# Decaying attention with a soft mixture of experts: the order of the turns in the score half of a pass, and a copy of the tokens' turns

## The chip, the cores and the metric

The kernel runs on one core of a Trainium2 chip, in one launch. The metric is the device time of an execution in microseconds. A core has TensorE (matrix products, here PE, and PEld for its weight loads), VectorE (DVE), ScalarE (ACT), GpSimd (POOL) and SyncE (SP), which issues all DMAs of this kernel. Each engine takes its instructions in the order of the program and stops at one whose inputs or whose buffer isn't ready; a semaphore tells it when they are. Products land in PSUM, which has 8 banks of 512 f32 columns on 128 partitions.

## The reference

All of it is computed in f32 (products partly in the fp32r form, with a second product for the low part):

```python
# attention: q, k, v [8, 8, 576, 64], f [8, 8, 576]
scores = q @ k.T / sqrt(64)
cum = cumsum(log(clip(f, 1e-4, 1)), -1)
scores = where(causal, -1e9, scores + cum[..., :, None] - cum[..., None, :])
attn = exp(scores - scores.max(-1))
attn = attn / (attn.sum(-1) + 1e-9)
x = (attn @ v).transpose(0, 2, 1, 3).reshape(4608, 512)
# soft mixture of experts: phi [512, 32], w1 [8, 512, 1024], w2 [8, 1024, 512]
logits = x @ phi
d = exp(logits - logits.max(0)); d /= d.sum(0) + 1e-9      # over tokens
slot_input = (d.T @ x).reshape(8, 4, 512)
slot_out[e] = relu(slot_input[e] @ w1[e]) @ w2[e]          # for each expert
c = exp(logits - logits.max(1)); c /= c.sum(1) + 1e-9      # over slots
out = c @ slot_out
```

## The kernel before

The 64 heads go through in 32 pairs, g = 0 to 31, four pairs to a batch of 576 tokens. Pair 0 has code of its own; pairs 1 to 31 run through the loop at line 714, one pass each, and its body is an order written out by hand: the lines are issued to the engines as they stand. In a pass the kernel

- makes the scores of the pair's heads h0 = 2g and h1 = 2g + 1 with keys on partitions (`s2`: two products for a segment, into three banks `ring` in turn), takes their exponential on ScalarE out of the bank (`expo`, one for each of four banks of a head) and lets GpSimd mask the diagonal blocks (`causal`);
- makes, between these, another form of scores for heads u0 = 2g + 3 and u1 = 2g + 4, with queries on partitions (`s1`, into three banks `s` in turn), out of which VectorE takes each query's maximum (`tops`: a masked maximum and then a reading of the accumulator). TensorE transposes the maxima of pair g + 1 (`mturn`, when u0's are there), ScalarE copies them (`mrows`), and a DMA puts them as a row into the operand `YA`, so that `s2` of the next pass subtracts them;
- turns the outcome of the pair before, g - 1: `px` transposes the five blocks of 128 tokens (t = 0 to 4, the last of 64 tokens) from tokens to channels, into two banks, `pv[0]` (blocks 0 and 3) and `pv[1]` (blocks 1, 2 and 4), and `xcopy` copies them on ScalarE to `XT`. These are the turns of channels;
- ends with 100 value products (`s3`) into the same two banks, `pv[0]` for h0 and `pv[1]` for h1, and `norm` on VectorE divides them by their sums, which frees the banks.

Columns 325 to 452 of these banks, beside the values, hold further small things: block 4's turn in `pv[1]`, and in `pv[0]` the transposes of `mturn` and `mtop`.

```python
    TURN = {0: (0, 0), 1: (1, 0), 2: (1, 128), 4: (1, 325), 3: (0, 128)}
```

The experts' routing of batch b is spread over the four passes behind it, by w = (g - 4) mod 4: in w = 0 the logits are made (`logits`, behind `s3`); in w = 1 their running maximum (`weigh`, `mgroup`, `mtop`, `mcast`) and the exponentials (`weigh2`), and behind `s3` `tokens` turns the logits (160 columns) and the negated maxima (32 columns) to tokens on partitions, into one of the three `s` banks. In w = 2 VectorE reads that bank: `combine(b, 0)` takes the maximum over the slots and subtracts it (lines 502 and 503), `shift` adds the maxima to the logits (468 and 470), and ScalarE takes the exponential (471); `dispatch` multiplies the outcome `LD` with the tokens in 40 products ahead of `s3`. In w = 3 the combining weights are made ready. Passes with w = 0 and 3 and the first three have nothing of this between the first score product and `s3`.

SP's queue loads values, queries and keys for later passes and in passes 5 to 27 a 512 KB quarter of the experts' weights each. From pass 28 on the buffers of the attention become free one by one, and the other weights are loaded into them (`wstream`). Behind the loop come the last batch's routing, the experts and the output.

Of the kernel before, what the change touches and what calls it, by code (L numbers as in the profile page):

```python
# [72 lines left out]
def attn_softmoe(ctx: ExitStack, tc: tile.TileContext, qk, v, f, phi, w1, w2, cst, out):  # L73
# [41 lines left out]

    mk = const.tile([P, NE], F32, name="mk")
    one = const.tile([1, 4], F32, name="one")
    under = const.tile([P, NS], F32, name="under")
    MT = [const.tile([P, 2 * NBLK], F32, name=f"MT{i}") for i in range(3)]


# [95 lines left out]
    def s1(i, *which):  # L217

        if not head(i):
            return  # L220
        g, h = divmod(i, 2)
        ya, wa, m = YA[g % 3], WA[g % 3][:, S * h : S * h + S], TOP[g % 3]
        for n in which:
            bank, o, blk, j0, w = TOPS[n]
            if o == 0:
                st["top", i % 2, bank] = scratch(False, f"s{i}_{bank}")
            t = st["top", i % 2, bank]
            nc.tensor.matmul(  # L228
                t[:, o : o + w], ya[0:m, h, 128 * blk : 128 * blk + 128], wa[0:m, j0 : j0 + w], start=True, stop=True
            )  # L230

    def tops(i, *which):
        if not head(i):
            return
        g, h = divmod(i, 2)
        for n in which:
            bank, o, blk, j0, w = TOPS[n]
            t = st["top", i % 2, bank]
            m0 = max(448 - (128 * blk + 64) + j0, 0)
            top = MT[g % 3][:, NBLK * h + blk : NBLK * h + blk + 1] if g else m2[h][:, blk, 1:2]  # L240
            nc.vector.tensor_tensor_reduce(  # L241
                out=t[:, o : o + w], in0=t[:, o : o + w], in1=mask[:, m0 : m0 + w], scale=1.0, scalar=top if n == 3 else -3.0e38,
                op0=ALU.add, op1=ALU.max, accum_out=top,
            )
# [20 lines left out]
    def s2(i, *which):  # L265
        if not head(i):
            return
        g, h = divmod(i, 2)
        ya, wa, yb, wb, m = YA[g % 3], WA[g % 3], YB[g % 2], WB[g % 2], TOP[g % 3] + 1
        for n in which:  # L270
            bank, c, i0, w = SEGS[n]
            t, at = (turn(), 0) if n < 4 else st["bank"]

            n = 128 if c < 4 else 64
            o = t[0:n, at : at + w]
            at += w
            j0 = S * h + 128 * c
            nc.tensor.matmul(o, wa[0:m, j0 : j0 + n], ya[0:m, h, 64 + i0 : 64 + i0 + w], start=True, stop=False)  # L278
            nc.tensor.matmul(o, wb[:, j0 : j0 + n], yb[:, h, i0 : i0 + w], start=False, stop=True)  # L279
            st["bank"] = t, at  # L280
# [80 lines left out]
    def px(g, t):  # L361
        if pair(g):
            n, o = TURN[t]
            turned(pv[n][:, o : o + 128], g, t)

    def xcopy(g, ts):
        if pair(g):
            n, o = TURN[ts[0]]
            if ts[0] == 4:
                return last(g, 128, pv[n][:, o : o + 128], nc.scalar.copy)  # L370
            w = 128 * len(ts)
            to = 64 + 128 * ts[0] if ts[0] else 0
            nc.scalar.copy(XT[g % NPAIR][:, to : to + w], pv[n][:, o : o + w])  # L373
# [73 lines left out]
    def tokens(b, *ns):  # L447
# [12 lines left out]
        if 1 in ns:  # L460
            nc.vector.tensor_copy(LD, pm[:, 160:320].rearrange("p (t s) -> p t s", t=NBLK))

    def shift(b):

        if not 0 <= b < B - 1:
            return
        pm = st["tok", b]
        nc.vector.tensor_copy(under, pm[:, 160:192])
        top = under.rearrange("p (o s) -> p o s", o=1).broadcast_to([P, NBLK, NS])
        nc.vector.tensor_tensor(LD, pm[:, 0:160].rearrange("p (t s) -> p t s", t=NBLK), top, op=ALU.add)  # L470
        nc.scalar.activation(LD, LD, AF.Exp)

    def dispatch(b, *ts):
        if not batch(b):
# [18 lines left out]
    def combine(b, step):  # L493

        if not batch(b):
            return
        ce = ctok[:, b]
        if step == 0:

            lt = st["tok", b][:, 0 : NBLK * NS].rearrange("p (t s) -> p t s", t=NBLK)  # L500
            sm = st["sm", b] = const.tile([P, 2, NBLK], F32, name=f"sm{b}", tag="sm", bufs=1)
            nc.vector.tensor_reduce(sm[:, 0], lt, axis=AX.X, op=ALU.max)
            nc.vector.tensor_tensor(ce, lt, wide(sm[:, 0]), op=ALU.subtract)
        elif step == 1:
            st["ce"] = turn()
            nc.scalar.activation(st["ce"][:, 0 : NBLK * NS].rearrange("p (t s) -> p t s", t=NBLK), ce, AF.Exp)
        else:
            sm, pm = st["sm", b], st["ce"]
            et, to = pm[:, 0 : NBLK * NS].rearrange("p (t s) -> p t s", t=NBLK), pm[:, NBLK * NS : NBLK * NS + NBLK]
            nc.vector.tensor_reduce(to, et, axis=AX.X, op=ALU.add)  # L510
            nc.vector.tensor_scalar_add(sm[:, 1], to, EPS)
            nc.vector.reciprocal(sm[:, 1], sm[:, 1])
            nc.vector.tensor_tensor(ce, et, wide(sm[:, 1]), op=ALU.mult)
# [200 lines left out]
    for g in range(1, NG):  # L714
        h0, h1 = 2 * g, 2 * g + 1
        u0, u1 = h0 + 3, h0 + 4
        b, w = divmod(g - 4, NPAIR)
        load_v(g + 1)
        load_qk(g + 3)
        if g >= 5 and g - 5 < NRES:  # L720
            wload(g - 5)
        if w == 1:
            weigh(b)
        low_q(h0 + 2)
        low_q(h1 + 2)
        s2(h0, 0)
        expo(h0, 0)
        norm(h0 - 1)
        if w == 1:
            mgroup(b)  # L730
        if w == 2:
            combine(b, 0)
            shift(b)
        s1(u0, 2)
        tops(u0, 2)
        s2(h0, 1)
        expo(h0, 1)
        s1(u0, 3)
        tops(u0, 3)
        s2(h0, 2)  # L740
        expo(h0, 2)
        px(g - 1, 0)
        s1(u0, 0, 1)
        tops(u0, 0, 1)
        s2(h0, 3)
        px(g - 1, 3)
        xcopy(g - 1, (0,))
        s2(h0, 4)
        s1(u0, 4, 5)
        s2(h0, 5)  # L750
        expo(h0, 3)
        xcopy(g - 1, (3,))
        tops(u0, 4, 5)
        causal(h0)
        low_k(h0 + 2)
        if w == 1:
            mtop(b)
        s2(h1, 0)
        expo(h1, 0)
        px(g - 1, 1)  # L760
        s1(u1, 2)
        tops(u1, 2)
        s2(h1, 1)
        px(g - 1, 2)
        expo(h1, 1)
        s1(u1, 3)
        tops(u1, 3)
        s2(h1, 2)
        xcopy(g - 1, (1, 2))
        px(g - 1, 4)  # L770
        expo(h1, 2)
        mturn(g + 1)
        mrows(g + 1)
        s1(u1, 0, 1)
        tops(u1, 0, 1)
        xcopy(g - 1, (4,))
        s2(h1, 3, 4)
        s1(u1, 4, 5)
        s2(h1, 5)
        expo(h1, 3)  # L780
        tops(u1, 4, 5)
        causal(h1)
        low_k(h1 + 2)
        load_cum(g + 3)
        dup_q(g + 2)
        dup_k(g + 2)
        if g == 29:
            sides[2].close()
            p2 = fresh(ctx, "p2", 2)
            wstream(RAW[30 % 3], *p2)  # L790
        if g == 30:
            sides[1].close()
            xp = ctx.enter_context(tc.tile_pool(name="xp", bufs=1))
            X.append(xp.tile([P, NBLK, 256], F32, name="X3"))
            p0 = fresh(ctx, "p0", 1)
            p1 = fresh(late, "p1", 3)
            wstream(RAW[31 % 3], *p0, *p1)
        if g == 31:
            sides[0].close()
            with tc.using_default_side("right"):  # L800
                tp = ctx.enter_context(tc.tile_pool(name="tp", bufs=1))
            cT = tp.tile([P, 4 * S], F32R, name="cT")
            wstream(tp.tile([P, QW], F32, name="p3"))
        if w == 1:
            mcast(b)
        if w == 3:
            combine(b, 1)
        if w == 2 and b < B - 2:
            dispatch(b, *range(NBLK))
        if g == NG - 1:  # L810
            st["lg", B - 1] = scratch(False, f"lg{B - 1}")
            nc.vector.memset(st["lg", B - 1][:, 128:192], -1.0e30)
        round_k(g + 3)
        if w == 1:
            weigh2(b)
            total(b)
        round_q(g + 3)
        if w == 3:
            combine(b, 2)
        s3(g, VALUES[:29])  # L820
        norm(h0)
        if g == 31:
            wstream(PTS[:, 0:QW])
            split(0, 0)
            split(1, 0)
        s3(g, VALUES[29:])
        if w == 0:
            logits(b, *range(NPAIR))
        if w == 1:
            tokens(b, 0)  # L830
        if g == 28:
            wstream(RAW[29 % 3])
# [263 lines left out]
```

## Time and profile before

| | |
|---|---|
| median of 3 runs | 421.94 us (421.42 to 423.97) |
| the profiled execution | 425.3 us, span 423.6 us |
| granted TensorE clock, mean | 0.976 |
| busy: PE, DVE, ACT, POOL | 90%, 68%, 65%, 59% |
| chain that ended last | PE 70%, ACT 12%, DVE 7%, DMA 5% |

The span is the time from the first to the last instruction of the profiled execution. The loop's passes 1 to 31 fill it up to 351.6 us; the routing of the last batch, the experts and the output come behind. In the rows of a timeline, instructions of one line that follow each other without a gap stand in one row with their count, and what stands in brackets is the idle time of the engine ahead of the row and what ended it. Engines overlap neighbouring instructions, so that one can start before the end of the one ahead of it.

### The profile page before, as it was taken

The numbers are of one execution on the slowest core, as the hardware profiler recorded it, in microseconds if no ns is written. First come the engines' busy times: TensorE is split into PE (matmuls) and PEld (weight loads), VectorE is DVE, ScalarE is ACT, GpSimd is POOL, SyncE is SP. The second block draws the span as 40 slices with busy tenths as digits, with TensorE's granted clock in tenths as the row PEclk, the third lists the DMA queues.
The fourth block names the chain that finished last, engine by engine and source line by source line (L and its number), as shares of the span: only waits on it lengthen the run. The fifth ranks groups of instructions, "written<-read, shape, count | busy, mean of one in ns | idle before, by whom it ended". The sixth has DMA issues, their size and how long they took to land.

```text
span 423.6 us, 15255 instructions
## 1 busy us (share of the span) xinstructions
PE 383.0 (90%) x5872; PEld 331.0 (78%) x5872; DVE 287.2 (68%) x1144; ACT 276.2 (65%) x693; POOL 250.8 (59%) x339
## 2 busy tenths in 40 slices
PE   8989998999899989998999999999999989999860
PEld 7878997889788979888888888888888886544530
DVE  7878776878677865787778677867786716412551
ACT  8868776767686765686868686868686663110541
POOL 3689877777677764787678767876787651010000
PEclk9999999999999997999999999999999999999985
DMA  6766556666666665577567756775665669999998
GB/s 203 222 171 181 149 148 196 196 195 198 195 197 195 198 195 159 162 216 241 152 187 213 237 157 153 241 231 166 184 197 142 185 224 381 342 411 409 353 352 318
DMA packets 35144, 93.72 MB, mean 221 GB/s; under 512 B 4234, under 2 KB 10048, under 8 KB 35072
## 3 DMA queue, kind: packets, MB, share of 16 engines
q1 hardware_dynamic: 35072, 92.75, 70.8%
q8 instruction: 46, 0.75, 0.7%
q14 instruction: 26, 0.21, 0.2%
HBM read 63.93 MB, written 9.73 MB: 174 GB/s over the span
## 4 chain that ended last, share of the span: by engine, by line
PE 70%; ACT 12%; DVE 7%; DMA 5%; issue 3%; SPq 0%; ACTq 0%; POOL 0%; DVEq 0%; POOLq 0%
PE pv L311 23%; PE s L228 9%; PE ring L278 9%; ACT PTS L285 8%; PE ring L279 8%; PE pv L338 4%; ACT XT L373 3%; PE lg L385 3%; DVE s L241 3%; DMA w<-in_w 2%; PE pv L946 2%; PE ds L482 2%; PE ring L909 2%; PE pv L909 2%; PE ring L519 2%
## 5 line engine op out<-in xcount | busy, mean ns | idle before, releaser
L285 ACT ACTIVATE PTS<-ring 128x320 f32<-128x320 f32 (+2 forms) x256 | 124.2, 513 | 61.5 <-PE ring L279 58.0
L241 DVE CUSTOM_DVE_ANT_0 s<-s,mask 128x320 f32<-128x320 f32 (+4 forms) x320 | 137.1, 451 | 20.0 <-PE s L228 15.0
L278 PE MATMUL ring<-YA,WA 67*128 67x320 f32 (+9 forms) x384 | 118.9, 321 | 0.0
L279 PE MATMUL ring<-YB,WB 128*128 128x320 f32 (+4 forms) x384 | 111.3, 298 | 0.0
L311 PE MATMUL pv<-V,PTS 128*64 128x65 f32 x3200 | 103.3, 225 | 0.3 <-ACT mr L260 0.3
L228 PE MATMUL s<-WA,YA 66*128 66x288 f32 (+9 forms) x384 | 101.4, 320 | 2.3 <-DVE LD L470 1.2
L311 PEld LDWEIGHTS pv<-V,PTS 128*64 128x64 f32 x3200 | 98.6, 140 | 2.9 <-issue 1.2
L207 POOL TENSOR_TENSOR WB<-RAW,WB 64x576 fp32r<-64x576 f32 x64 | 90.3, 1411 | 16.3 <-DMA WB<-WA 6.3
L212 POOL TENSOR_TENSOR YB<-RAW,YA 64x576 fp32r<-64x576 f32 x64 | 89.5, 1417 | 2.5
L278 PEld LDWEIGHTS ring<-YA,WA 67*128 67x128 f32 (+3 forms) x384 | 69.3, 182 | 5.6 <-issue 2.1
L279 PEld LDWEIGHTS ring<-YB,WB 128*128 128x128 f32 (+1 forms) x384 | 70.2, 183 | 0.0
L228 PEld LDWEIGHTS s<-WA,YA 66*128 66x128 f32 (+1 forms) x384 | 63.5, 192 | 8.4 <-PE ring L279 2.9
L296 POOL TENSOR_SCALAR_AFFINE_SELECT PTS<-PTS 128x128 f32<-128x128 f32 (+1 forms) x128 | 31.3, 265 | 50.9 <-ACT PTS L285 50.5
L338 PE MATMUL pv<-cs,X 128*128 128x128 f32 x155 | 44.1, 284 | 12.3 <-ACT XT L373 11.7
L241 DVE DVE_READ_ACCUMULATOR2_ANT MT<- 128x1 f32 x372 | 52.7, 142 | 0.0
L293 POOL TENSOR_SCALAR_AFFINE_SELECT PTS<-PTS 128x384 f32<-128x384 f32 x64 | 33.3, 521 | 30.9 <-ACT PTS L285 28.4
L181 ACT CAST WA<-RAW 64x576 fp32r<-64x576 f32 x64 | 40.0, 668 | 0.8
L186 ACT CAST YA<-RAW 64x576 fp32r<-64x576 f32 x64 | 40.0, 669 | 0.4
L241 DVE CUSTOM_DVE_ANT_0 s<-s,mask,MT 128x288 f32<-128x288 f32 x62 | 32.6, 526 | 10.3 <-PE s L228 1.4
L338 PEld LDWEIGHTS pv<-cs,X 128*128 128x128 f32 x155 | 21.9, 141 | 21.6 <-ACT XT L373 20.0
L326 DVE TENSOR_SCALAR rl<-pv 128x5 f32<-128x5 f32 x64 | 10.5, 164 | 39.5 <-PE pv L311 29.3
L331 DVE TENSOR_TENSOR X<-pv,rl 128x320 f32<-128x320 f32 (+1 forms) x65 | 31.5, 486 | 2.4 <-DVE rl L327 0.3
(209 smaller groups left out, 375.8 us busy)
## 6 DMA issues: line engine op xcount, KB each, us to landing
w<-in_w SPq DMA_DIRECT2D x46, 512.0 KB
RAW<-in_qk SPq DMA_DIRECT2D x31, 576.0 KB
V<-in_v SPq DMA_DIRECT2D x32, 325.0 KB
WB<-WA SPq DMA_DIRECT2D x31, 288.0 KB
YB<-YA SPq DMA_DIRECT2D x31, 288.0 KB
p<-in_w SPq DMA_DIRECT2D x7, 512.0 KB
out<-RAW SPq DMA_DIRECT2D x12, 256.0 KB
out<-p SPq DMA_DIRECT2D x5, 512.0 KB
```

Source lines behind the costliest of these rows:

```text
L181: nc.scalar.copy(WA[g % 3][0:64, S * h : S * h + S], RAW[g % 3][64:128, h])
L186: nc.scalar.copy(YA[g % 3][0:64, h, 64:640], RAW[g % 3][0:64, h])
L207: nc.gpsimd.tensor_tensor(t[0:64], RAW[g % 3][64:128, h], t[64:128].bitcast(F32), op=ALU.subtract)
L212: nc.gpsimd.tensor_tensor(YB[g % 2][64:128, h], RAW[g % 3][0:64, h], YA[g % 3][0:64, h, 64:640].bitcast(F32), op=ALU.subtract)
L228: nc.tensor.matmul(t[:, o : o + w], ya[0:m, h, 128 * blk : 128 * blk + 128], wa[0:m, j0 : j0 + w], start=True, stop=True)
L241: nc.vector.tensor_tensor_reduce(out=t[:, o : o + w], in0=t[:, o : o + w], in1=mask[:, m0 : m0 + w], scale=1.0, scalar=top if n == 3 else ...
L278: nc.tensor.matmul(o, wa[0:m, j0 : j0 + n], ya[0:m, h, 64 + i0 : 64 + i0 + w], start=True, stop=False)
L279: nc.tensor.matmul(o, wb[:, j0 : j0 + n], yb[:, h, i0 : i0 + w], start=False, stop=True)
L285: nc.scalar.activation(PT[i % 2][:, SEG_O[bank] : SEG_O[bank] + at], t[:, 0:at], AF.Exp, scale=0.125)
L293: nc.gpsimd.affine_select(d3, d3, pattern=[[0, 3], [1, 128]], compare_op=ALU.is_ge, fill=0.0, base=0, channel_multiplier=-1)
L311: nc.tensor.matmul(pvv[h][64 * u : 64 * u + 64, t, :], PT[h][:, at : at + 64], V[:, g % 2, c, 65 * h : 65 * h + 65], start=(c == 0), stop= ...
L338: nc.tensor.transpose(pm[:, 0:128], x[:, t, 128 * (p % 2) : 128 * (p % 2) + 128], ident)
```

## The change

The order of a pass is changed in two ways. First, the turns: block 3 is turned ahead of `s2(h0, 3)` and not behind it, blocks 1 and 2 in the first head's half and not the second's, block 4 behind `s2(h1, 0)` and not behind `s2(h1, 2)`. The copy of block 3 stands ahead of `expo(h0, 3)`, the copies of blocks 1 and 2 and of block 4 stand together between `expo(h1, 0)` and `expo(h1, 1)`. The number of turns and copies is the same. Second, in passes with w = 2, VectorE copies all 192 columns of the tokens' turns to SBUF in one go (`keep`, tile `TK`), which takes the place of the copy of 32 columns; `combine(b, 0)` and `shift` read the copy and are issued later, and the exponential of `LD` (`grow`) is parted from `shift` and stands behind `expo(h1, 1)`.

```diff
--- before.py
+++ after.py
@@ -115,7 +115,7 @@
 
     mk = const.tile([P, NE], F32, name="mk")
     one = const.tile([1, 4], F32, name="one")
-    under = const.tile([P, NS], F32, name="under")
+    TK = const.tile([P, 192], F32, name="TK")
     MT = [const.tile([P, 2 * NBLK], F32, name=f"MT{i}") for i in range(3)]
 
 
@@ -460,15 +460,20 @@
         if 1 in ns:
             nc.vector.tensor_copy(LD, pm[:, 160:320].rearrange("p (t s) -> p t s", t=NBLK))
 
+    def keep(b):
+        if 0 <= b < B - 1:
+            nc.vector.tensor_copy(TK, st["tok", b][:, 0:192])
+
     def shift(b):
 
         if not 0 <= b < B - 1:
             return
-        pm = st["tok", b]
-        nc.vector.tensor_copy(under, pm[:, 160:192])
-        top = under.rearrange("p (o s) -> p o s", o=1).broadcast_to([P, NBLK, NS])
-        nc.vector.tensor_tensor(LD, pm[:, 0:160].rearrange("p (t s) -> p t s", t=NBLK), top, op=ALU.add)
-        nc.scalar.activation(LD, LD, AF.Exp)
+        top = TK[:, 160:192].rearrange("p (o s) -> p o s", o=1).broadcast_to([P, NBLK, NS])
+        nc.vector.tensor_tensor(LD, TK[:, 0:160].rearrange("p (t s) -> p t s", t=NBLK), top, op=ALU.add)
+
+    def grow(b):
+        if 0 <= b < B - 1:
+            nc.scalar.activation(LD, LD, AF.Exp)
 
     def dispatch(b, *ts):
         if not batch(b):
@@ -497,7 +502,7 @@
         ce = ctok[:, b]
         if step == 0:
 
-            lt = st["tok", b][:, 0 : NBLK * NS].rearrange("p (t s) -> p t s", t=NBLK)
+            lt = (TK if b < B - 1 else st["tok", b])[:, 0 : NBLK * NS].rearrange("p (t s) -> p t s", t=NBLK)
             sm = st["sm", b] = const.tile([P, 2, NBLK], F32, name=f"sm{b}", tag="sm", bufs=1)
             nc.vector.tensor_reduce(sm[:, 0], lt, axis=AX.X, op=ALU.max)
             nc.vector.tensor_tensor(ce, lt, wide(sm[:, 0]), op=ALU.subtract)
@@ -729,27 +734,32 @@
         if w == 1:
             mgroup(b)
         if w == 2:
-            combine(b, 0)
-            shift(b)
+            keep(b)
         s1(u0, 2)
         tops(u0, 2)
         s2(h0, 1)
         expo(h0, 1)
         s1(u0, 3)
         tops(u0, 3)
+        if w == 2:
+            combine(b, 0)
         s2(h0, 2)
         expo(h0, 2)
         px(g - 1, 0)
         s1(u0, 0, 1)
         tops(u0, 0, 1)
+        if w == 2:
+            shift(b)
+        px(g - 1, 3)
         s2(h0, 3)
-        px(g - 1, 3)
+        px(g - 1, 1)
         xcopy(g - 1, (0,))
+        xcopy(g - 1, (3,))
         s2(h0, 4)
+        px(g - 1, 2)
         s1(u0, 4, 5)
         s2(h0, 5)
         expo(h0, 3)
-        xcopy(g - 1, (3,))
         tops(u0, 4, 5)
         causal(h0)
         low_k(h0 + 2)
@@ -757,23 +767,23 @@
             mtop(b)
         s2(h1, 0)
         expo(h1, 0)
-        px(g - 1, 1)
+        px(g - 1, 4)
+        xcopy(g - 1, (1, 2))
+        xcopy(g - 1, (4,))
         s1(u1, 2)
         tops(u1, 2)
         s2(h1, 1)
-        px(g - 1, 2)
         expo(h1, 1)
+        if w == 2:
+            grow(b)
         s1(u1, 3)
         tops(u1, 3)
         s2(h1, 2)
-        xcopy(g - 1, (1, 2))
-        px(g - 1, 4)
         expo(h1, 2)
         mturn(g + 1)
         mrows(g + 1)
         s1(u1, 0, 1)
         tops(u1, 0, 1)
-        xcopy(g - 1, (4,))
         s2(h1, 3, 4)
         s1(u1, 4, 5)
         s2(h1, 5)
```

## Rows read from the trace of the kernel before

**Rows 1.** Waits of TensorE: who waited for whom, us in total, times, longest us.

```profile
PE pv L338 <- ACT XT L373: 11.7, 31, 0.6
PE pv L411 <- ACT XT L373: 6.5, 7, 0.9
...
PE pv L311 <- ACT mr L260: 0.3, 1, 0.3
```

**Rows 2.** Timeline, TensorE, pass g = 15: start us, us, engine, line, operation.

```profile
178.71 0.34 PE L278 MATMUL ring<-YA,WA 98*128 98x192 f32 x1
178.88 0.28 PE L279 MATMUL ring<-YB,WB 128*128 128x192 f32 x1
...
180.81 0.31 PE L279 MATMUL ring<-YB,WB 128*128 128x320 f32 x1
181.49 0.33 PE L338 MATMUL pv<-cs,X 128*128 128x128 f32 x1 [0.38 <-ACT XT L373]
181.66 0.27 PE L251 MATMUL pv<-cs,MT 128*10 128x128 f32 x1
...
182.29 0.25 PE L278 MATMUL ring<-YA,WA 98*128 98x192 f32 x1
182.38 0.27 PE L279 MATMUL ring<-YB,WB 128*128 128x192 f32 x1
...
182.96 0.28 PE L311 MATMUL pv<-V,PTS 128*64 128x65 f32 x2
```

**Rows 3.** Timeline, ScalarE, the same pass.

```profile
179.64 0.60 ACT L285 ACTIVATE PTS<-ring 128x512 f32<-128x512 f32 x1 [0.39 <-PE ring L279]
180.14 0.26 ACT L373 COPY XT<-pv 128x128 f32<-128x128 f32 x1
180.28 0.89 ACT L285 ACTIVATE PTS<-ring 128x448 f32<-128x448 f32 x2
181.03 0.41 ACT L373 COPY XT<-pv 128x256 f32<-128x256 f32 x1
181.28 0.50 ACT L285 ACTIVATE PTS<-ring 128x320 f32<-128x320 f32 x1
182.01 0.26 ACT L260 CAST mr<-pv 10x128 fp32r<-10x128 f32 x1 [0.23 <-ACT PTS L285]
182.18 0.41 ACT L344 COPY XT<-pv 64x64 f32<-64x64 f32 x2
```

**Rows 4.** Timeline, VectorE, the same pass: last reading of u0's maxima.

```profile
180.66 0.14 DVE L241 DVE_READ_ACCUMULATOR2_ANT MT<- 128x1 f32 x1
```

**Rows 5.** Timeline, TensorE, pass g = 17 (w = 1), at `mtop`.

```profile
199.43 0.22 PE L279 MATMUL ring<-YB,WB 128*64 128x64 f32 x1
200.58 0.27 PE L411 MATMUL pv<-cs,mb 128*1 128x128 f32 x1 [0.93 <-ACT XT L373]
```

**Rows 6.** Timeline, VectorE, pass g = 18 (w = 2).

```profile
208.41 0.32 DVE L502 TENSOR_REDUCE sm<-tk 128x5 f32<-128x160 f32 x1
...
209.22 0.33 DVE L470 TENSOR_TENSOR LD<-tk,under 128x160 f32<-128x160 f32 x1
...
212.38 0.14 DVE L241 DVE_READ_ACCUMULATOR2_ANT MT<- 128x1 f32 x1
```

**Rows 7.** Timeline, TensorE, the same pass: the maxima's transpose.

```profile
213.23 0.27 PE L251 MATMUL pv<-cs,MT 128*10 128x128 f32 x1
```

**Rows 8.** Instructions of line 404: count, ns min/median/max, first and last start, shapes.

```profile
L404 DVE TENSOR_REDUCE mb<-LGM x7: 354/355/356, 67.7 to 323.7; 128x1 f32<-128x193 f32 x7
L404 DVE TENSOR_REDUCE mb<-lg x1: 357/357/357, 355.3 to 355.3; 128x1 f32<-128x192 f32 x1
```

**Rows 9.** Windows: us, PE, PEld, DVE, ACT, POOL busy, clock, DMA share, GB/s.

```profile
176.76:186.10 9.34, 8.96 (x144) 8.40 (x143) 8.08 (x34) 7.19 (x19) 6.38 (x10) 1.00 0.59 188
157.60:164.45 6.85, 6.85 (x98) 6.66 (x100) 2.59 (x14) 4.86 (x13) 3.91 (x6) 0.50 0.43 84
360.00:370.00 10.00, 9.94 (x150) 5.54 (x154) 3.79 (x14) 1.39 (x5) 0.18 (x1) 1.00 0.98 342
```

## Prediction

> **What bounds the kernel now.** I read the waits of TensorE first, because it is busy 90% of the span and a wait there is lost time unless something else is later still. Nearly all its idle time inside the 31 loop passes has two causes, and both are ScalarE copies out of the banks that the turns go into: 11.7 us before a turn, in all 31 passes, and 6.5 us before the transpose of `mtop`, in 7 passes [rows 1]. Then I read one pass without extra work engine by engine, pass g = 15, 9.34 us long [rows 9]. On TensorE the reader is to see one stop: the turn of block 4 starts 0.68 us after the product ahead of it (180.81 to 181.49), then everything runs on to the first value product at 182.96 [rows 2]. On ScalarE, the copy of blocks 1 and 2 runs from 181.03 to 181.44, and the turn starts 0.05 us behind it [rows 3]. Turn 4 writes columns that this copy doesn't read; it waits because they lie in the same bank. So the order of turns and copies in the two banks is what costs, not the amount of work.
>
> **What the edit does to the first wait.** Passes 1 to 31 issue as many turns and copies as before, so nothing is added; only places change. Turn 4 now stands ahead of the copies of its bank, and behind them no TensorE work goes to that bank until the value products. The wait is gone. Its worth lies between the idle time, 0.38 us, and the start-to-start time less what the product ahead needs. A product of 192 columns passes in 0.09 us (182.29 to 182.38) [rows 2], so 320 columns in 0.15 us, and the loss is 0.68 - 0.15 = 0.53 us. I take 0.53: the idle time is counted from the modelled end of the product ahead, the loss from its start, and products follow each other by their starts.
>
> **What is late next in a plain pass.** Two turns more (blocks 1 and 2) stand ahead of the last score products of the first head. A turn costs TensorE 0.08 us (0.17 us from 178.71 to 178.88 with a turn ahead, 0.09 without one) plus 0.03 of its own start: 0.11 us, between 0.08 and 0.17 [rows 2]. So the last bank of that head is ready 0.22 us later, and its exponential starts at 179.86 and not 179.64. From there I follow ScalarE in its new order, with the starts of [rows 3]: 0.50 us to the next exponential (180.36), 0.44, half of the 0.89 us that two exponentials take, to the copy of blocks 1 and 2 (180.80), 0.25 to the two half copies of block 4 (181.05), 0.41 for these (181.46), then two exponentials of 320 columns, each 0.50 long and overlapping by 0.14, as the second of that pair and the copy behind it do (end at 182.32), then the copy of the maxima, 0.26 long, which ends at about 182.46. This copy reads the bank into which the first value product goes, and that product has waited for it once already [rows 1]. TensorE, 0.53 us earlier, would be ready at 182.43, so it waits about 0.07 us: a plain pass gains 0.46 us. The bounds: 0.53 if the copy isn't late; if no ScalarE instruction overlaps the next, its seven take 0.60 + 0.60 + 0.41 + 0.41 + 0.50 + 0.50 + 0.26 = 3.28 us from 179.86, the product starts at 183.19, and the pass loses 0.23 us. The neighbours in [rows 3] do overlap, so I stay near the first.
>
> VectorE has to be done with the maxima of the first head, u0, before their transpose: the last reading ends at 180.80 [rows 4]; the transpose, at 181.66 now [rows 2], would want it at 181.13. It holds, with 0.33 us to spare. The copy of block 3 goes ahead of an exponential where ScalarE had 0.39 us idle [rows 3], so it costs nothing; without that idle time it would add 0.2 us to the chain above. GpSimd's masks and the DMA of the maxima on SP's queue follow the same instructions as before, at most some tenths later, and the rows that they bring are read only in the next pass.
>
> **Passes with `mtop`** (w = 1, 7 of them). The transpose starts 1.15 us after the product ahead of it, 0.93 of that idle [rows 5]; it waits for the copy of block 3, which stands behind an exponential of 0.60 us. After the edit that copy stands ahead of this exponential, done when the product is. Between 0.93 and 1.1 us come back; I take 1.0. Together with turn 4's 0.53 it makes 1.53, less 0.08 for small waits: 1.45 us. ScalarE isn't late here, since the transpose and the broadcast of the new maximum lengthen TensorE's path.
>
> **Passes with the tokens' turns** (w = 2, 7 of them). VectorE works through four operations in a row, from 208.41 to 209.55 (the first and the last of them in [rows 6]), ahead of the first maxima. The edit replaces one, a copy of 32 columns, with a copy of 192 columns, and puts two behind the second maxima and one behind the third. The large copy lies between nothing and 0.36 us, the time of a reduction of 192 columns [rows 8]; against the short one I take 0.18 us more. What stood ahead of the maxima now stands between them, so the last reading, which ends at 212.52 now, ends at about 212.70 (212.5 to 212.9) [rows 6]. The maxima's transpose needs it, and can start at 212.8 instead of 213.23 [rows 7]: here the removed wait turns into a wait for VectorE, and the gain is only 0.4 us (0.2 to 0.55). The exponential of LD no longer stands ahead of two others; its new place delays the copy of the maxima by 0.34 us, which the 40 dispatch products hide.
>
> [...]
>
> **The sum.** Plain passes (w = 0 and 3, and the first three) are 17: 17 x 0.46 = 7.8 us. 7 x 1.45 = 10.2 us. 7 x 0.4 = 2.8 us. In all 20.8 us. The tail behind the loop is bound by the weights' stream (DMA share 0.98) [rows 9], but that stream starts when the loop frees its buffers, so the tail moves with the loop and doesn't shrink. The profiled execution took 425.3 us, and would take 404.5. [...] On the median, 421.9 - 20.8 = 401.1; some of the new small waits I will have missed, so I say 402.
>
> **Rivals.** *VectorE takes over the wait in plain passes too.* The maxima's transpose has 0.33 us to spare; if the moved turns push the second half of u0's products and VectorE 0.5 us later, 0.2 us a pass is lost again (24 passes, 4.8 us): about 407. For it: VectorE is busy for 8.1 of the 9.34 us of that pass [rows 9]. Against: at that point it works off a queue, so that products that come 0.22 us later still find it busy.
>
> *ScalarE becomes the bound* through the chain without overlaps: 17 passes lose 0.23 (3.9 us), the `mtop` passes keep 1.0 (7 us), the others 0.4 (2.8 us): 422 - 5.9 = 416. Against it: the neighbours in [rows 3] that don't wait overlap.
>
> *The edit doesn't do what it says.* Only turn 4 comes free and `mtop` still waits for a copy: 402 + 6.5 = 408. If both still wait, 421; nothing in the new order would make them.
>
> [...]
>
> **Chances.** Forecast (398 to 406) 0.66; VectorE 0.15; `mtop` still waiting 0.05; ScalarE 0.07; no change 0.03; slower 0.04. The lower end is all waits gone with nothing in their place (17 x 0.53 + 7 x 1.6 + 7 x 0.55 = 24.1 us: 398); the upper takes in the VectorE and `mtop` cases and small bounds on top, 412. About 0.86 lies inside. The runs before spread over 0.6%, so 1% (4.2 us) is about what can be told from no change. Faster by over 1% are all cases but the last two, 0.93; of the last two 0.04 is slower and 0.03 the same.
>
> **What the profile after would show.** Right: no wait of the turns and of `mtop` for the XT copies; no ScalarE wait for LD; plain passes of 8.8 to 8.9 us where g = 15 has 9.34 us (the transpose of the maxima near 4.5 us after the pass's first product); a new, short wait of the transpose for VectorE in 7 passes; perhaps a wait of the first value product for the maxima's copy. Wrong: waits of 0.2 us or more at that product in the plain passes (ScalarE), or before the transpose in all passes (VectorE), or a clock of 0.5 in several stretches.

## The result, and the profile after

The changed kernel takes 397.51 us (median of 4 runs, 396.58 to 398.76) where the kernel before, in its 4 runs of this comparison, takes 422.96 (421.42 to 424.11): ratio 0.940 (95% interval 0.936 to 0.945). The forecast was 402 with a range from 398 to 412: the direction and the mechanism came out, the gain was 25 us and not 20, and the time lies half a microsecond below the range. In this document ratios leave out the runs that took over 1.5% longer than the fastest of their kernel, at a lower granted clock (0.962 to 0.967), while medians and ranges have them in.

The page of the profile after, its span, the busy time of TensorE and the chain that ended last:

```profile
span 396.3 us, 15220 instructions
...
PE 372.3 (94%) x5872; PEld 326.3 (82%) x5872; DVE 284.0 (72%) x1144; ACT 272.0 (69%) x693; POOL 250.9 (63%) x339
...
PE 74%; DVE 9%; DMA 9%; POOL 3%; ACT 1%; issue 1%; SPq 1%; DVEq 0%; POOLq 0%; ACTq 0%
```

TensorE is busy for 94% of the span, and ScalarE's share of the chain has fallen from 12% to 1%. The waits of TensorE after the change (who waited for whom, us in total, times, longest):

```profile
PE pv L251 <- DVE MT L241: 3.1, 7, 0.6
...
PE pv L311 <- ACT mr L260: 0.2, 1, 0.2
```

The two lines of [rows 1] that cost 11.7 and 6.5 us are gone altogether. In their place stand 3.1 us in which the transpose of the maxima waits for VectorE, in the 7 passes with w = 2, as the prediction had it. The wait of the first value product for the copy of the maxima is listed with 0.2 us, where it was 0.3; its small share in the plain passes isn't in this list, as the timeline below shows.

Four stretches of the kernel before: one pass each with w = 0, 1 and 2 (g = 16 to 18), counted from the end of one pass's value products to the end of the next, and the part behind the loop. Behind the window stand its length, the busy time of PE, PEld, DVE, ACT and POOL, the granted TensorE clock, the DMA share and GB/s:

```profile
186.10:195.44 9.34, 8.98 (x146) 8.40 (x150) 7.31 (x30) 7.50 (x19) 7.66 (x11) 1.00 0.77 225
195.44:207.43 11.99, 10.76 (x185) 9.66 (x184) 8.17 (x34) 8.12 (x24) 7.82 (x11) 1.00 0.62 178
207.43:218.90 11.47, 10.94 (x187) 9.79 (x186) 8.64 (x35) 8.64 (x21) 8.71 (x12) 1.00 0.69 197
351.60:423.60 72.00, 54.73 (x728) 30.43 (x727) 26.88 (x76) 18.29 (x51) 2.37 (x8) 0.91 0.99 366
```

The same four stretches of the changed kernel:

```profile
171.40:180.17 8.77, 8.77 (x147) 8.37 (x150) 7.20 (x30) 6.32 (x18) 7.64 (x11) 1.00 0.83 240
180.17:190.50 10.33, 10.33 (x184) 9.58 (x184) 7.87 (x34) 8.87 (x25) 7.74 (x11) 1.00 0.70 204
190.50:201.50 11.00, 10.59 (x186) 9.68 (x186) 8.69 (x35) 8.53 (x21) 8.75 (x12) 1.00 0.78 212
324.02:396.32 72.30, 55.43 (x728) 30.58 (x727) 26.94 (x77) 18.32 (x51) 2.37 (x8) 0.90 0.98 365
```

The passes take 8.77, 10.33 and 11.00 us where they took 9.34, 11.99 and 11.47, and TensorE is busy without a gap in the first two. The part behind the loop takes 72.3 us, as before (72.0): it moved ahead with the loop. With 17 plain passes and 7 of either other kind the loop gives 17 x 0.57 + 7 x 1.66 + 7 x 0.47 = 24.6 us. The two spans differ by 27.3 us. Pass 13 of the execution before, which has the stretch at half clock [rows 9], takes 15.02 us where the other passes with w = 1 take 11.99, so that stretch cost 3.0 us; the execution after has none in its loop (granted clock 1.00 up to 324 us). Added up pass by pass, and without those 3.0 us, the loop gives 24.1 us, since not every pass is typical: pass 1 gains 0.05 us. In the second profiled execution of the changed kernel, further down, pass 1 gains 0.56, and the sum is 24.6.

The timeline of TensorE after the change, in a plain pass (g = 16, first product at 171.33), at the transpose of `mtop` (g = 17), and at the transpose of the maxima in g = 18:

```profile
171.33 0.47 PE L278 MATMUL ring<-YA,WA 67*128 67x448 f32 x1
...
175.53 0.31 PE L279 MATMUL ring<-YB,WB 128*128 128x320 f32 x1
175.68 0.27 PE L251 MATMUL pv<-cs,MT 128*10 128x128 f32 x1
...
177.03 0.39 PE L311 MATMUL pv<-V,PTS 128*64 128x65 f32 x5
...
184.34 0.22 PE L279 MATMUL ring<-YB,WB 128*64 128x64 f32 x1
184.40 0.27 PE L411 MATMUL pv<-cs,mb 128*1 128x128 f32 x1
...
195.13 0.31 PE L279 MATMUL ring<-YB,WB 128*128 128x320 f32 x1
195.85 0.28 PE L251 MATMUL pv<-cs,MT 128*10 128x128 f32 x1 [0.41 <-DVE MT L241]
```

The transpose of the maxima (line 251) follows the product ahead of it by 0.15 us (175.53 to 175.68); before, 0.85 us lay between them, turn 4 with its wait among it [rows 2]. It starts 4.35 us after the pass's first product, where the prediction had about 4.5; in g = 15 before it was 4.97 (176.69 to 181.66). The first value product follows it by 1.35 us (175.68 to 177.03), and before by 1.30 (181.66 to 182.96, [rows 2]). The transpose of `mtop` follows its product by 0.06 us, where it took 1.15 [rows 5]. In g = 18 the wait that took the place of the old one is to be seen: 0.41 us for VectorE's last reading.

ScalarE in the same plain pass:

```profile
174.46 1.03 ACT L285 ACTIVATE PTS<-ring 128x512 f32<-128x512 f32 x2 [0.64 <-PE ring L279]
175.38 0.38 ACT L373 COPY XT<-pv 128x256 f32<-128x256 f32 x1
175.63 0.44 ACT L344 COPY XT<-pv 64x64 f32<-64x64 f32 x2
176.09 0.77 ACT L285 ACTIVATE PTS<-ring 128x320 f32<-128x320 f32 x2
176.74 0.24 ACT L260 CAST mr<-pv 10x128 fp32r<-10x128 f32 x1
```

This is the chain that the prediction followed: from the exponential of the first head's last bank at 174.46, through the copies of blocks 1, 2 and 4, to the copy of the maxima, which ends at 176.98, 2.52 us later, where the prediction had 2.60. The value product starts at 177.03, right behind it: the 0.05 us that it comes later behind the transpose than before is this wait (0.05 to 0.09 us in the other plain passes), close to the 0.07 of the prediction. The list of waits doesn't have it, because idle time is counted there from the modelled end of the product ahead.

VectorE in g = 18, the copy of 192 columns (line 465), the two operations of `combine` (507, 508), the one of `shift` (472) and the last reading ahead of the transpose:

```profile
191.41 0.35 DVE L465 COPY TK<-tk 128x192 f32<-128x192 f32 x1
...
192.87 0.32 DVE L507 TENSOR_REDUCE sm<-TK 128x5 f32<-128x160 f32 x1
193.23 0.53 DVE L508 TENSOR_TENSOR ctok<-TK,sm 128x160 f32<-128x160 f32 x1
...
194.55 0.32 DVE L472 TENSOR_TENSOR LD<-TK 128x160 f32<-128x160 f32 x1
...
195.65 0.14 DVE L241 DVE_READ_ACCUMULATOR2_ANT MT<- 128x1 f32 x1
```

The copy takes 0.35 us, 0.17 more than the copy of 32 columns before (0.18), and the prediction took 0.18 more. The subtraction of line 508 takes 0.53 us; the same operation took 0.32 when it read the tokens' turns from their bank (the second of the four operations that begin in [rows 6]; a row of it, of the same length, stands in the last section). More on that below.

### The profile page after: what moved, and what is told of

It is laid out like the page before. It is cut to its first block, busy times and chain, and to the rows that moved or that the text cites. A ratio compares the mean times of both kernels' runs of the same rounds, so it can differ in the third digit from the quotient of the medians.

```text
span 396.3 us, 15220 instructions
## 1 busy us (share of the span) xinstructions
PE 372.3 (94%) x5872; PEld 326.3 (82%) x5872; DVE 284.0 (72%) x1144; ACT 272.0 (69%) x693; POOL 250.9 (63%) x339
## 4 chain that ended last, share of the span: by engine, by line
PE 74%; DVE 9%; DMA 9%; POOL 3%; ACT 1%; issue 1%; SPq 1%; DVEq 0%; POOLq 0%; ACTq 0%
PE pv L311 24%; PE ring L278 12%; PE ring L279 10%; PE s L228 10%; DMA w<-in_w 5%; DVE s L241 4%; PE pv L338 3%; PE lg L385 3%; PE ds L487 2%; PE pv L919 1%; PE ring L919 1%; DMA out<-p 1%; POOL WB L207 1%; PE pv L956 1%; PE pv L251 1%
## 5 line engine op out<-in xcount | busy, mean ns | idle before, releaser
L285 ACT ACTIVATE PTS<-ring 128x320 f32<-128x320 f32 (+2 forms) x256 | 118.2, 502 | 53.2 <-PE ring L279 39.8
L311 PE MATMUL pv<-V,PTS 128*64 128x65 f32 x3200 | 101.7, 223 | 1.2 <-POOL PTS L293 0.8
L311 PEld LDWEIGHTS pv<-V,PTS 128*64 128x64 f32 x3200 | 96.9, 138 | 5.0 <-issue 1.2
L338 PE MATMUL pv<-cs,X 128*128 128x128 f32 x155 | 42.1, 273 | 0.6 <-DVE X L331 0.6
L373 ACT COPY XT<-pv 128x128 f32<-128x128 f32 (+1 forms) x93 | 25.2, 306 | 1.1 <-PE pv L338 0.8
```

What stands on the lines that cost most here:

```text
L285: nc.scalar.activation(PT[i % 2][:, SEG_O[bank] : SEG_O[bank] + at], t[:, 0:at], AF.Exp, scale=0.125)
L311: nc.tensor.matmul(pvv[h][64 * u : 64 * u + 64, t, :], PT[h][:, at : at + 64], V[:, g % 2, c, 65 * h : 65 * h + 65], start=(c == 0), stop= ...
L338: nc.tensor.transpose(pm[:, 0:128], x[:, t, 128 * (p % 2) : 128 * (p % 2) + 128], ident)
```

## Experiments

**The turns alone.** The new order of turns and copies, with VectorE's part as before:

```diff
 (against the changed kernel)
-        if w == 2: keep(b)
+        if w == 2: combine(b, 0); shift(b)      # both as in the kernel before
...
-        if w == 2: combine(b, 0)
-        if w == 2: shift(b)
-        if w == 2: grow(b)
```

> The new order of turns and ScalarE copies alone; VectorE's work on the tokens' turns and the exponential of LD stay as they were before. Theory (the gain is the two bank waits): plain passes 8.77 us and w = 1 passes 10.32 as after the whole change. In w = 2 passes VectorE does its four operations ahead of the maxima (1.14 us) and not 0.35 + 0.32 + 0.53 + 0.32 us between them, so the last reading comes earlier and the maxima's transpose waits about 0.2 us less than after the whole change: passes of 10.8, time 396 us (395 to 397.5). Rival (the copy of the tokens' turns carries part of the gain): w = 2 passes stay near 11.3 to 11.45, time 400 to 401. Rival (the clock): no loss of time can be seen in the passes, time near 420.

Measured: 395.66 us (395.41 to 400.83, 6 runs) beside 421.25 for the kernel before on that chip, ratio 0.942 (0.936 to 0.947). Passes with w = 0 and 2:

```profile
170.70:179.47 8.77, 8.76 (x147) 8.37 (x150) 7.20 (x30) 6.18 (x17) 7.67 (x11) 1.00 0.83 240
...
189.79:200.53 10.74, 10.63 (x186) 9.70 (x186) 8.38 (x35) 8.48 (x21) 8.74 (x12) 1.00 0.74 207
```

The turns carry the whole gain, and the passes with w = 2 take 10.74 us, less than with the whole change (11.00). So the copy of the tokens' turns, placed as the change places it, costs 0.26 us in each of six such passes, about 1.5 us (the seventh, pass 30, has no dispatch products and doesn't lose). The times of whole executions hardly tell these two kernels apart: this one's ratio, 0.936 to 0.947, overlaps with that of the changed kernel on the same chip below. It is the passes that show it.

**The copy alone.** VectorE's part of the change in the old order of turns:

```diff
 (against the kernel before)
-        if w == 2: combine(b, 0); shift(b)
+        if w == 2: keep(b)
...
+        if w == 2: combine(b, 0)      # behind tops(u0, 3)
+        if w == 2: shift(b)           # behind tops(u0, 0, 1)
+        if w == 2: grow(b)            # behind expo(h1, 1)
```

> VectorE's copy of the tokens' turns, with the later combine, shift and exponential, alone; turns and ScalarE copies as before. Theory: plain passes 9.34 us and w = 1 passes 11.99 as before, since both bank waits stand. In w = 2 passes the wait of the first maxima for the fourth operation goes (0.4 us), and the exponential of LD, now ahead of the copy of blocks 1 and 2, gives most of it back at turn 4: 11.2 to 11.4 us, time 420.5 to 422 where before has 422 (ratio 0.995 to 1.0). Rival (the copy carries part of the gain): 0.5 us or more in each w = 2 pass, 418 or less.

Measured: 420.11 us (418.54 to 424.2, 12 runs) beside 421.25, ratio 0.9985 (0.995 to 1.002), which is no difference. Waits of TensorE, and a pass with w = 2:

```profile
PE pv L338 <- ACT XT L373: 12.9, 31, 0.8
PE pv L411 <- ACT XT L373: 6.5, 7, 0.9
```

```profile
202.47:213.69 11.22, 10.74 (x186) 9.72 (x186) 8.82 (x35) 8.57 (x21) 8.80 (x12) 1.00 0.71 203
```

Both bank waits stand, the first longer than before (12.9 us where it was 11.7): the exponential of LD now stands ahead of the copy that turn 4 waits for, and part of what VectorE gives at the front of the pass goes there: the pass above takes 11.22 us where the one before took 11.47.

**The whole change, with `combine` and `shift` later.**

```diff
 (against the changed kernel)
         tops(u0, 3)
-        if w == 2: combine(b, 0)
...
         tops(u0, 0, 1)
-        if w == 2: shift(b)
...
         tops(u0, 4, 5)
+        if w == 2: shift(b)
...
         tops(u1, 4, 5)
+        if w == 2: combine(b, 0)
```

> The whole change, with shift issued behind the first head's last maxima and combine behind the second head's last maxima. Theory: the wait of the maxima's transpose for VectorE (0.41 us in each w = 2 pass) comes from the two operations of combine and the one of shift that stand between the maxima; with them behind, the transpose doesn't wait, w = 2 passes take 10.55 to 10.65 us and the time is 394.5 us (394 to 395.5). If shift and the exponential of LD are then late for the dispatch products, a wait of up to 0.2 us shows there. Rival (the w = 2 passes are bound by TensorE or ScalarE already, the wait would only move): 11.0 us, time 397.5.

Measured: 394.15 us (393.66 to 396.31, 6 runs), ratio 0.936 (0.932 to 0.940), 3.4 us below the changed kernel on the same chip. A pass with w = 2:

```profile
189.24:199.67 10.43, 10.43 (x186) 9.74 (x186) 9.54 (x35) 8.47 (x21) 8.81 (x12) 1.00 0.73 208
```

TensorE is busy for all of the 10.43 us, and the wait for VectorE is gone from the list. So that wait came from the three operations between the maxima, and with the copy in SBUF there is freedom to put them where nobody waits; the change had the freedom and didn't use it to the end.

**The changed kernel again**, on the chip of these three:

> The changed kernel once more, on the same chip as the three others: ratio 0.940 (0.936 to 0.945), time 397 to 398 us, plain passes 8.77, w = 1 10.32, w = 2 11.0 us. If the stretch at half clock inside the loop had been part of the kernel before and not of this one, the ratio stays; if it comes by chance, single executions of both kernels differ by some 2 to 3 us.

Measured: 397.56 us (396.72 to 402.58, 6 runs), ratio 0.945 (0.940 to 0.950). The ratio lies at the upper end of what was expected, since the kernel before takes 421.25 us on this chip; the typical passes repeat to 0.03 us. A low clock is no property of the kernel before: among the profiled executions the one before has its stretch at half clock (at 157.6 us), with a mean granted clock of 0.976, and that of the copy alone has a mean of 0.977, that of the second swap below one of 0.962, where the changed kernel's two have 0.982 and 0.981. But one of the six runs here, at 402.58 us, had a mean granted clock of 0.970 where the others had 0.980 to 0.984, so the changed kernel isn't free of it either. What brings it no run shows.

**The first wait by itself.** One swap in the kernel before:

```diff
+        px(g - 1, 4)
         xcopy(g - 1, (1, 2))
-        px(g - 1, 4)
```

> The kernel before with one swap: the turn of block 4 stands ahead of the copy of blocks 1 and 2. Theory: this is the first wait by itself, in all 31 passes. By the prediction's price (0.53 us) plain passes take 8.81 us; by what the passes after the whole change show (0.57 net, about 0.62 for the wait alone) they take 8.72 to 8.77. Passes with w = 1 take 11.4, with the second wait still there; w = 2 about 10.9 to 11.0. Time 403 to 405 us beside 421 of before. Rival (the turns and copies must all move, or ScalarE's or VectorE's order takes the gain back): plain passes above 9.1, time above 412.

Measured: 404.68 us (404.01 to 405.28, 4 runs) beside 420.86, ratio 0.961 (0.959 to 0.963). Passes with w = 0 and 1, and the turn of block 4 in the first of them, with the products around it:

```profile
175.44:184.20 8.76, 8.76 (x147) 8.45 (x150) 7.25 (x31) 6.95 (x18) 7.67 (x11) 1.00 0.83 240
184.20:195.66 11.46, 10.54 (x185) 9.70 (x184) 8.17 (x34) 8.63 (x25) 7.80 (x11) 1.00 0.65 185
```

```profile
179.51 0.31 PE L279 MATMUL ring<-YB,WB 128*128 128x320 f32 x1
179.66 0.27 PE L338 MATMUL pv<-cs,X 128*128 128x128 f32 x1
179.77 0.27 PE L251 MATMUL pv<-cs,MT 128*10 128x128 f32 x1
```

One swapped pair of lines gives 16 us of the 25. A plain pass takes 8.76 us, 0.58 to 0.60 less than 9.34, where the prediction had priced the wait at 0.53. The pass with w = 1 takes 11.46 us, 0.53 less.

**The second wait by itself.** Another swap in the kernel before:

```diff
+        xcopy(g - 1, (3,))
         expo(h0, 3)
-        xcopy(g - 1, (3,))
```

> The kernel before with one swap: the copy of block 3 stands ahead of the exponential of the first head's last bank. Theory: this is the second wait by itself. Passes with w = 1 lose 1.0 to 1.1 us (10.9 to 11.0 where before has 11.99), all others stay (9.34, 11.45); time 413.5 to 414.5 us beside 421. Rival (the transpose of mtop would wait for something else next, VectorE's maximum for example): w = 1 passes above 11.5, time above 417.

Measured: 411.89 us (410.7 to 419.16, 4 runs) beside 420.86, ratio 0.978 (0.976 to 0.980). A plain pass and one with w = 1:

```profile
186.26:195.49 9.23, 8.98 (x147) 8.41 (x150) 7.30 (x30) 7.57 (x19) 7.66 (x11) 1.00 0.78 228
154.66:165.66 11.00, 10.69 (x185) 9.65 (x184) 7.93 (x34) 8.08 (x24) 7.80 (x11) 1.00 0.68 195
```

The pass with w = 1 falls by 0.99 us, as expected. The time is some 2 us below what was expected, because the plain passes fell too, by 0.1 us (9.23): the copy of block 3 no longer stands between the exponential and the copy that turn 4 waits for, so that wait gets shorter (8.8 us in all, where it was 11.7). The wait of `mtop` is not quite gone here: its transpose still comes 0.17 us behind the product ahead of it (199.47 to 199.65 in g = 17), and 0.06 with the whole change. The profiled execution is the one of 419.16 us, with a mean granted clock of 0.962; in both passes shown the clock is 1.00. The two swaps alone, 16.2 us and 9.2 (without that execution), add to 25.4; the turns as a whole gave 25.6 on the other chip.

**Bank or order.** The order of the kernel before, with the small columns of the two banks changed over:

```diff
-    TURN = {0: (0, 0), 1: (1, 0), 2: (1, 128), 4: (1, 325), 3: (0, 128)}
+    TURN = {0: (0, 0), 1: (1, 0), 2: (1, 128), 4: (0, 325), 3: (0, 128)}
```

Besides, `mturn` in the loop and `mtop` write `pv[1][:, 325:453]` in place of `pv[0][:, 325:453]`.

> The kernel before, its order untouched: the turn of block 4 goes to the free columns 325 to 452 of the bank of blocks 0 and 3, and the transposes of the maxima and of mtop go to these columns of the bank of blocks 1 and 2. Theory (a product waits for a ScalarE copy when it writes the same bank, whatever the columns): the turn of block 4 no longer waits, and the transpose of the maxima right behind it waits for the copy of blocks 1 and 2 in its place, so plain passes stay at 9.3 us (9.2 to 9.4); mtop writes a bank that nobody copies from at that point, so w = 1 passes lose 1.0 to 1.1 us; time 413.5 to 415 us. Rival (the wait comes from the order of ScalarE's queue or from what the turn reads, not from the bank): the turn of block 4 still waits in 31 passes, mtop still waits 0.9 us, time 421.

Measured: 414.53 us (413.98 to 422.59, 4 runs) beside 420.86, ratio 0.984 (0.983 to 0.986). Waits of TensorE; the turn of block 4 and the transpose of the maxima in a plain pass, with the product ahead of them; `mtop` and the turn of block 1 in a pass with w = 1; the windows of these two passes:

```profile
PE pv L251 <- ACT XT L373: 7.9, 30, 0.5
PE pv L338 <- DVE row L412: 5.3, 7, 0.8
```

```profile
183.20 0.31 PE L279 MATMUL ring<-YB,WB 128*128 128x320 f32 x1
183.35 0.27 PE L338 MATMUL pv<-cs,X 128*128 128x128 f32 x1
183.88 0.28 PE L251 MATMUL pv<-cs,MT 128*10 128x128 f32 x1 [0.25 <-ACT XT L373]
```

```profile
192.28 0.22 PE L279 MATMUL ring<-YB,WB 128*64 128x64 f32 x1
192.34 0.28 PE L411 MATMUL pv<-cs,mb 128*1 128x128 f32 x1
...
193.77 0.33 PE L338 MATMUL pv<-cs,X 128*128 128x128 f32 x1 [0.75 <-DVE row L412]
```

```profile
179.13:188.29 9.16, 8.91 (x147) 8.35 (x150) 7.31 (x30) 7.51 (x19) 7.66 (x11) 1.00 0.79 231
188.29:199.99 11.70, 10.75 (x185) 9.49 (x184) 8.02 (x34) 8.03 (x24) 7.82 (x11) 1.00 0.63 180
```

Turn 4, in the other bank, doesn't wait for the copy (0.15 us behind its product), and the transpose behind it, which now writes the bank of that copy, does, in 30 passes. `mtop` doesn't wait either (192.28 to 192.34). That is the bank, not the order and not what is read. Each bank here is one buffer of the program, so these runs can't part the two; and what TensorE waits for is a semaphore, so no run shows what the chip would do without it. Half of the expectation failed, though: the passes with w = 1 lost 0.3 us and not 1.0, since the turn of block 1, behind `mtop` in the same bank, now waits 0.75 us for VectorE to read the outcome of `mtop`. That the time came out as expected is luck: the plain passes are 0.18 us shorter, since only one instruction, and not two, now stands behind the end of that copy (7.9 us of waiting in all, where it was 11.7).

## Why the prediction was off

**The mechanism was right.** It named the two waits, said that the bank makes them, that VectorE's reading takes the place of the first in 7 passes and that the copy of the maxima comes a little late in the others. The two swaps show the waits, one by one; the bank swap shows the bank; the list of waits after and the late `shift` show VectorE's reading; the timelines of ScalarE and TensorE show the copy.

**What failed is the size of the terms**, first of all the prices of the two waits. In the sum, 7.8 us for the plain passes were 9.7 (17 x 0.57); 10.2 us for those with `mtop` were 11.6 (7 x 1.66); 2.8 us for those with the tokens' turns were 3.3 (7 x 0.47). That is 24.6 and not 20.8, and 421.94 - 24.6 = 397.3, within 0.2 us of the measured time (397.8 with the 24.1 us of that execution's passes). The 0.9 us that were added for missed waits make up the rest of the miss.

- *The price of turn 4's wait.* The step took the time to the turn's start, 0.68 us less 0.15, and let everything behind it run as usual. With the swap alone, in which nothing waits, the turn follows its product by 0.15 us and the transpose follows the turn by 0.11 (179.51, 179.66, 179.77): 0.26 us in all, where it was 0.68 and 0.17, 0.85 in all [rows 2]. So the wait cost 0.59 us: 0.53 ahead of the turn, as priced, and 0.06 behind it, which the price left out. The passes with the swap alone are 0.58 to 0.60 us shorter. With the whole order of turns 0.62 us are gained up to the transpose (4.97 to 4.35), and the late copy of the maxima takes 0.05 back.
- *The price of `mtop`'s wait.* The step took 1.0 us out of 0.93 to 1.1. The transpose follows its product by 0.06 us now and by 1.15 before: 1.09, and with 0.57 for turn 4 that is the 1.66 measured. By the same distance from start to start the price was there to read.
- *The small waits.* The 0.07 us in each plain pass were about right (0.05 to 0.09). The 0.08 us in the `mtop` passes were not there: from the transpose of the maxima to the first value product they take 1.47 us before and after (g = 17), as the prediction's own remark on ScalarE there had said. The last 0.9 us had no row behind them at all; without them the forecast would have been 401.
- *The lower end.* It priced all waits as gone with nothing in their place, with the same 0.53 us a pass: 24.1 us. A bound worked out with the value of a term and not with the bound of that term is no bound. From the kernel's own rows the price could have been bounded by the whole distance between the product and the transpose, 0.85 us, less one product and one turn, 0.15 and 0.11: 0.59, which is what was measured. With it the lower end would have been 17 x 0.59 + 7 x 1.69 + 7 x 0.55 = 25.7 us below 421.9, at 396.

**The passes with the tokens' turns** came out as said (0.47 for 0.4), in part by luck. Counted from the pass's first product, the last reading of the maxima ended after 4.66 us in g = 18 (207.86 to 212.52) and ends after 4.87 (190.92 to 195.79): 0.21 later, where the prediction had 0.18. It had those from the larger copy alone, which did add its 0.17. The subtraction of line 508 added another 0.21, 0.53 us instead of 0.32, and 0.17 came back elsewhere in VectorE's queue, which isn't explained here; the prediction had neither. Its sum has no term for reading from SBUF instead of the bank, and reductions of one tensor take as long from either (354 to 357 ns, [rows 8]). The subtraction has two tensors, both now in SBUF, and in each of its 7 passes a mask of GpSimd was running when it started (last section). With the turns alone the last reading ends after 4.59 us (190.21 to 194.80), and the 0.28 us between are about what the passes of the whole change lose against that run (0.26). No run takes the 0.21 away by itself.

**The rivals.** VectorE as the wait of the plain passes: none there, in 17 passes. `mtop` still waiting: no. ScalarE's chain without overlaps: 2.52 us against 3.28. A slower kernel, with a clock of 0.5 in several stretches: none in the loop of the profiled execution after, and the second one of the changed kernel has the same mean granted clock (0.981 beside 0.982), with TensorE busy for 94% of the span and not 90%.

## What to carry to other kernels

Where a bank is shared between several small results, look at who reads it last before each product: in this kernel a product that writes other columns still stops behind that read (up to 0.6 us at the turn of block 4, up to 0.9 at the transpose of `mtop`), and a swap of two lines in the order can be worth 4% of a kernel whose TensorE is 90% busy. Price such a wait by the whole distance that it opens between the instructions around it, not by the idle time that is shown in front of one (0.59 us here, where 0.38 was shown). And move the work that a copy out of a bank sets free to where nobody waits for it: here, beside the turns alone, the copy cost about 1.5 us in the middle of the maxima and gained 1.5 at their end.

## What the hardware showed that was not expected

Beside a GpSimd operation that was running when it started, a VectorE operation that reads two tensors from SBUF took 0.53 us and not 0.32. In the changed kernel a mask of GpSimd starts 0.17 us before line 508 does (193.23 to 193.76, shown above), and ends 0.18 us before it ends; in all 7 passes it starts 0.15 to 0.17 us before and ends 0.17 to 0.18 us before, and the operation takes 0.53 to 0.54 us:

```profile
193.06 0.52 POOL L293 TENSOR_SCALAR_AFFINE_SELECT PTS<-PTS 128x384 f32<-128x384 f32 x1 [0.16 <-ACT PTS L285]
194.70 0.52 POOL L296 TENSOR_SCALAR_AFFINE_SELECT PTS<-PTS 128x128 f32<-128x128 f32 x2 [1.11 <-ACT PTS L285]
```

With `combine` at the end of the pass the same line meets a subtraction of GpSimd that is 1.41 us long:

```profile
197.10 1.20 DVE L508 TENSOR_TENSOR ctok<-TK,sm 128x160 f32<-128x160 f32 x1
```

```profile
196.71 1.41 POOL L207 TENSOR_TENSOR WB<-RAW,WB 64x576 fp32r<-64x576 f32 x1
```

GpSimd ends at 198.12, VectorE at 198.30, and the operation takes 1.20 us; over the 7 passes it takes 0.83 to 1.50 us. With the tokens' turns read from their bank, one tensor in PSUM and one in SBUF, the operation takes 0.32 to 0.33 us, in the kernel before also in the 6 of 7 passes in which a GpSimd operation runs all through it; in the experiment with the turns alone:

```profile
191.04 0.33 DVE L503 TENSOR_TENSOR ctok<-tk,sm 128x160 f32<-128x160 f32 x1
```

```profile
189.41 2.79 POOL L212 TENSOR_TENSOR YB<-RAW,YA 64x576 fp32r<-64x576 f32 x2
```

In `shift`, where VectorE started 0.15 us ahead of GpSimd (194.55 to 194.70), the operation took 0.32 us; with the late `shift` it took 0.43. What makes the operation longer beside GpSimd no run shows by itself: the rows show when the two ran and how long they took. That GpSimd is held up in its turn they hardly show: its masks behind `shift` take 0.31 to 0.32 us, where masks of that shape take 0.29 elsewhere.
